# An attention block interleaved with dense products: the order of the score products in each first visit, and the place of one output piece

## The chip, the cores and the metric

The kernel runs on one core of one Trainium2 chip. The metric is the device time of one launch in microseconds; a kernel's time is the median of its runs. TensorE is the matrix engine (PE in the profile, PEld its weight loads), VectorE is DVE, ScalarE is ACT, GpSimd is POOL, and SyncE (SP) issues the DMAs.

## The reference

A pre-normalised transformer layer on 2048 tokens of width 1024, in bfloat16. The attention has 32 heads of 32 columns and a sliding window of 256 keys:

```python
qkv = (x @ wqkv)                      # x here is layernorm(A_x); split into q, k, v by head
scores = einsum("bhqd,bhkd->bhqk", q, k) * (Dh ** -0.5)
mask = (i - j >= 0) & (i - j < 256)
p = softmax(where(mask, scores, -1e9))
h = A_x + einsum("bhqk,bhkd->bhqd", p, v).reshape(B, S, D) @ wo
out = h + silu(layernorm(h) @ w1) @ w2
```

`B_x` is not used: the second half works on `h`.

## The kernel before, in words

The tokens are cut into four blocks of 512. TensorE first makes v, q and k of block 0, then of blocks 1, 2 and 3, then the product with `wo`, then both dense layers of the second half. All of these are groups of eight products of 512 columns, 128 by 128 weights each, which accumulate into one bank of PSUM. Three banks (`four[0]` to `four[2]`) take turns through `next_acc`; a copy on VectorE (line 254 for v, 264 for q and k, an addition on line 285 for `wo`) empties the bank of a finished group. `four[3]`, also called `o_ps`, is kept for the attention's output.

The attention is pushed in between these products. `between` (line 464) is called ahead of each single product and counts them in `self.seen`; two tables written out in `Attention.__init__` say at which count a *visit* or a *piece* comes. From count 256 on there are twelve periods of 48 products. In a period that starts at count t there are:

- three visits, at t+4 (n = 0, the first), t+20 and t+36 (n = 2, the third);
- four pieces, at t+41, t+45, t+59 and t+76. The piece at t+41 is the first of the two behind the third visit, that at t+45 the second; the other two fall into the next period, at its counts 11 and 28.

The order of the program is the order of issue on each engine; the kernel's own schedule is kept.

**A visit** (line 329) makes scores for four heads. Each head has its own strip of 32 rows of the array, and each strip is used in two halves of 64 columns, so eight small products can be under way at once. A head's *own* scores go to the PSUM tile `sc` in parts of 320, 128 and 64 columns. Some heads also stream a second set of 512 columns into a *second bank*: one that is `idle`, the one `behind` (the bank of the group just finished, which VectorE's copy must have emptied) or `out` (`o_ps`, which the normalisation of the piece before must have read). In the first visit heads 0, 1 and 2 have the second banks `idle`, `out` and `behind`, each in four parts of 128 columns (`unit_c`), and head 3 has none. The list `todo` is sorted by `at`, the number of columns that a head has streamed so far, so that the heads advance side by side. There are 48 products in a first visit, 44 in a second and 36 in a third.

ScalarE then takes the exponentials: for the second banks first (line 315 in the first visit), then for `sc` (lines 321 and 322); GpSimd cuts the triangles (line 409).

**A piece** (`attn_piece`, line 442) makes the output of one pair of heads: 24 products of 33 columns into `o_ps` (line 419), and behind them on VectorE the normalisation, a reciprocal (line 430) and a product (line 431) that read `o_ps`. The next piece, and the next second bank `out`, must wait for line 431. Behind a second piece the finished pair is transposed by a DMA on SP (line 439), which `run_late` issues ahead of the next group.

The lines by which a visit builds its order are these:

```python
runs = [(sc[:, h, :], own[half])]
...
at = 0
for bank, parts in runs:
    for p in parts:
        todo.append((at, h, half, bank, p))
        at += p[3] - p[2]
todo.sort(key=lambda m: m[0])
```

Of the kernel before, what the change touches and what calls it, by code (L numbers as in the profile page):

```python
# [47 lines left out]
def kernel(  # L48
# [46 lines left out]
    four = [ps.tile([P, 512], F32, name=f"bank{i}") for i in range(4)]  # L95
# [31 lines left out]
    def xbuf(i):  # L127
        return r_e[:, 3072 + 5120 * (i % 2):5632 + 5120 * (i % 2)]

    def ybuf(i):  # L130
        return r_e[:, 5632 + 5120 * (i % 2):8192 + 5120 * (i % 2)]
# [168 lines left out]
    def unit_xy(i, odd):  # L300
        q0 = odd * P
        mid, first, last = odd, odd - 2, odd + 2
        return [
            [(i, mid, q0, q0 + 320, 64), (i, last, q0 + 256, q0 + 384, 384), (i, first, q0, q0 + 64, 0)],
            [(i, mid, q0 + 64, q0 + 384, 128), (i, first, q0, q0 + 128, 0), (i, last, q0 + 320, q0 + 384, 448)],
        ]

    def unit_c(i):
        pair = (i, i + 1) if (i + 1) % 3 < (i + 2) % 3 else (i + 1, i)
        return [[(ii, kt, q * P, q * P + P, (n * 2 + m) * P)  # L310
                 for n, ii in enumerate(pair) for m, (kt, q) in enumerate(((-1, 0), (2, 3)))]] * 2

    def exp_c(i, h, bank):
        lo, hi = sorted(((i + 1) % 3, (i + 2) % 3))
        nc.scalar.activation(out=c_ring[:, lo:hi + 1:hi - lo, h, :], in_=four[bank].rearrange("p (n q) -> p n q", q=256),  # L315
                             func=ACT.Exp, scale=scale)

    def exp_xy(e, banks, h0, h1):
        tri, mid = banks[:, :, 0:192], banks[:, :, 192:320]
        tri = bass.AP(tensor=tri.tensor, offset=tri.offset, ap=[*tri.ap[:2], [320, 2], tri.ap[2]])  # L320
        nc.scalar.activation(out=tri_of(e)[:, h0:h1, :, 64:256], in_=tri, func=ACT.Exp, scale=scale)  # L321
        nc.scalar.activation(out=full_of(e)[:, h0:h1, :], in_=mid, func=ACT.Exp, scale=scale)

    def select_xy(e, pair):
        four_q = e[:, 1024 * pair:1024 * (pair + 1)].rearrange("p (c q) -> p c q", q=256)
        select(four_q[:, :, 0:P], four_q[:, :, 64:64 + P], False)
        select(four_q[:, :, P:2 * P], four_q[:, :, P:2 * P], True)

    def visit(i, n):


        now = acc_n[0] % 3
        idle, behind, out = (now + 1) % 3, (now + 2) % 3, 3
        if n == 0:
            own, e_own = unit_xy(i, 0), xbuf(i)
            more = [(0, idle, unit_c(i)), (1, out, unit_c(i)), (2, behind, unit_c(i))]
        elif n == 1:
            own, e_own = unit_xy(i, 1), ybuf(i)
            more = [(3, idle, unit_c(i)), (0, out, unit_xy(i + 1, 0)), (1, behind, unit_xy(i + 1, 0))]
        else:  # L340
            own, e_own = unit_xy(i + 1, 1), ybuf(i + 1)
            more = [(2, out, unit_xy(i + 1, 0)), (3, behind, unit_xy(i + 1, 0))]
        todo = []
        for h in range(4):
            for half in range(2):
                runs = [(sc[:, h, :], own[half])]
                for hh, bank, unit in more:
                    if hh == h:
                        runs.append((four[bank], unit[half]))
                at = 0  # L350
                for bank, parts in runs:
                    for p in parts:
# [3 lines that stand above are left out]
        for _, h, half, bank, (ii, kt, qa, qb, col) in todo:  # L356
            b, g = divmod(ii, G)
            t = b * 4 + kt
            r0, k0 = h * DH, (t % 4) * P + half * 64
            nc.tensor.matmul(  # L360
                bank[half * 64:half * 64 + 64, col:col + qb - qa],
                lhsT=kT[t // 4][r0:r0 + DH, g, k0:k0 + 64], rhs=qT[b][r0:r0 + DH, g, qa:qb],
                start=True, stop=True, tile_position=(r0, half * 64),
            )
        side = [h for h, _, unit in more if len(unit[0]) == 3]
        for h, bank, unit in more:
            if h in side:
                exp_xy(xbuf(i + 1), four[bank].rearrange("p (h q) -> p h q", h=1), h, h + 1)
            else:
                exp_c(i, h, bank)  # L370
        if side:
            select_xy(xbuf(i + 1), side[0] // 2)
        exp_xy(e_own, sc[:], 0, 4)
        for pair in range(2):
            select_xy(e_own, pair)

    def scores_0(g, odd):

        q0 = odd * P
        parts = [  # L380
            (odd, 0, q0, q0 + 320, 0), (odd, 1, q0, q0 + 384, 0),
            (odd + 2, 0, q0 + 256, 448, 320), (odd + 2, 1, q0 + 320, 448, 384),
        ]
        if odd:
            parts = [(a, h, f, min(t, 512), c) for a, h, f, t, c in parts[:2]] + [
                (3, 0, 384, 512, 320), (3, 1, 448, 512, 384), (2, 0, 448, 512, 448), (2, 1, 448, 512, 448)]
        for step in range(0, len(parts), 2):
            for hh in range(4):
                for t, half, qa, qb, col in parts[step:step + 2]:
                    r0 = hh * DH  # L390
                    k0 = t * P + half * 64
                    nc.tensor.matmul(  # L392
                        sc[half * 64:half * 64 + 64, hh, col:col + qb - qa],
                        lhsT=kT[0][r0:r0 + DH, g, k0:k0 + 64],
                        rhs=qT[0][r0:r0 + DH, g, qa:qb],
                        start=True, stop=True, tile_position=(r0, half * 64),
                    )
        e = (ybuf if odd else xbuf)(g)[:, 0:2048].rearrange("p (h q) -> p h q", q=512)
        nc.scalar.activation(out=e[:, :, 0:256], in_=sc[:, :, 0:256], func=ACT.Exp, scale=scale)  # L399
        nc.scalar.activation(out=e[:, :, 320:512], in_=sc[:, :, 256:448], func=ACT.Exp, scale=scale)  # L400
        nc.scalar.activation(out=c_ring[:, (g + 1) % 3, :, 128 + 64 * odd:192 + 64 * odd], in_=sc[:, :, 448:512],
                             func=ACT.Exp, scale=scale)
        select(e[:, :, 0:P], e[:, :, 0:P], True)
        select(e[:, :, 256:384], e[:, :, 320:448], False)
        select(e[:, :, 384:512], e[:, :, 384:512], True)
# [42 lines left out]
    class Attention:  # L448


        def __init__(self):
            self.seen = 0
            self.visits, self.pieces = {}, {}
            for d in range(2 * G):
                self.visits[92 + 10 * d] = lambda d=d: scores_0(d // 2, d % 2)
                self.pieces[(122 + 10 * d, 267, 284)[max(d - 13, 0)]] = (d // 2, d % 2)
            for p in range((NB - 1) * G // 2):
                i, t = G + 2 * p, 256 + 48 * p
                for n in range(3):
                    self.visits[t + 4 + 16 * n] = lambda i=i, n=n: visit(i, n)  # L460
                for n in range(4):
                    self.pieces[t + (41, 45, 59, 76)[n]] = (i + n // 2, n % 2)

        def between(self, kt):
            if self.seen in self.pieces:
# [168 lines left out]
    for g0 in range(0, G, 4):  # L634
        for w in range(2):
            for g in range(g0, g0 + 4):
                run_late()
                n = g0 * 2 + w * 4 + g % 4
# [170 lines left out]
```

## Time and profile before

| what | value |
|---|---|
| median of 3 runs | 690.12 us (689.69 to 690.25) |
| time of the profiled execution | 690.01 us |
| its span, first to last instruction | 688.3 us |
| mean granted TensorE clock | 1.000 |
| PE busy | 674.4 us (98% of the span) |
| PEld busy | 338.1 us (49%) |
| DVE busy | 296.0 us (43%) |
| ACT busy | 237.8 us (35%) |
| POOL busy | 155.4 us (23%) |
| first score product of a visit to the last | 90.6 us to 265.7 us |

The span is 1.7 us shorter than the execution's own time; the rest lies ahead of the first and behind the last instruction. A row of a timeline gives the start of its first instruction, the time until the end of its last one, the engine, the line of the kernel, what is written and read, and how many instructions the row merges. A matmul's recorded duration runs from its issue to the end of its passage through the array, so neighbouring matmuls overlap: products of 512 columns last 379 ns in the records and start about 215 ns apart. A few per cent of the matmul records are missing from the trace: behind every score visit but one, and behind the second pieces, one product fewer is recorded than the program has there.

### The profile page before, as it was taken

The numbers are of one execution on the slowest core, as the hardware profiler recorded it, in microseconds if no ns is written. First come the engines' busy times: TensorE is split into PE (matmuls) and PEld (weight loads), VectorE is DVE, ScalarE is ACT, GpSimd is POOL, SyncE is SP. The second block draws the span as 40 slices with busy tenths as digits, with TensorE's granted clock in tenths as the row PEclk, the third lists the DMA queues.
The fourth block names the chain that finished last, engine by engine and source line by source line (L and its number), as shares of the span: only waits on it lengthen the run. The fifth ranks groups of instructions, "written<-read, shape, count | busy, mean of one in ns | idle before, by whom it ended". The sixth has DMA issues, their size and how long they took to land.

```text
span 688.3 us, 14482 instructions
## 1 busy us (share of the span) xinstructions
PE 674.4 (98%) x6099; PEld 338.1 (49%) x6200; DVE 296.0 (43%) x616; ACT 237.8 (35%) x412; POOL 155.4 (23%) x247
## 2 busy tenths in 40 slices
PE   9999999999999999999999999999999999999998
PEld 4445555555555555444444444444444444444445
DVE  5287745774444446733316133343233251333111
ACT  7356666666767664023300033300133100233000
POOL 1046656666676665000000000000000000000000
DMA  8823144124522687765023310023300124100110
GB/s 274 260 53 96 21 59 101 26 42 106 174 78 71 199 283 212 157 244 202 1 87 112 84 39 1 0 92 73 81 1 0 31 87 90 39 1 0 31 38 24
DMA packets 77617, 61.50 MB, mean 89 GB/s; under 512 B 52464, under 2 KB 60656, under 8 KB 77552
## 3 DMA queue, kind: packets, MB, share of 16 engines
q1 hardware_dynamic: 77408, 60.31, 31.3%
q8 instruction: 48, 0.79, 0.5%
q10 hardware_dynamic: 144, 0.26, 0.1%
q14 instruction: 17, 0.14, 0.1%
HBM read 39.85 MB, written 8.39 MB: 70 GB/s over the span
## 4 chain that ended last, share of the span: by engine, by line
PE 97%; issue 2%; DMA 1%; DVE 0%; SPq 0%; ACT 0%; ACTq 0%; DVEq 0%
PE hacc L728 16%; PE bank L262 16%; PE hacc L756 15%; PE bank L756 13%; PE bank L728 12%; PE bank L283 8%; PE bank L252 6%; PE bank L419 5%; PE sc L360 2%; PE bank L360 1%; PE bank L547 1%; PE sc L392 1%; DMA r_w<-in_A_wqkv_dram 1%; PE tp L252 1%; ACT r_e L321 0%
## 5 line engine op out<-in xcount | busy, mean ns | idle before, releaser
L409 POOL TENSOR_SCALAR_AFFINE_SELECT r_e<-r_e 128x512 bf16<-128x512 bf16 x240 | 152.5, 643 | 115.3 <-ACT r_e L399 52.4
L756 PEld LDWEIGHTS <-r_a 128*128 128x128 bf16 x952 | 90.9, 98 | 103.0
L728 PEld LDWEIGHTS <-r_w 128*128 128x128 bf16 x896 | 87.7, 98 | 105.7
L756 PE MATMUL hacc<-r_a 128*128 128x512 bf16 (+2 forms) x523 | 103.2, 356 | 0.5
L756 PE MATMUL bank<-r_a 128*128 128x512 bf16 x412 | 91.4, 379 | 0.5
L728 PE MATMUL hacc<-r_e,r_w 128*128 128x512 bf16 x375 | 84.4, 379 | 0.5
L262 PEld LDWEIGHTS <-r_w 128*128 128x128 bf16 x512 | 45.4, 97 | 49.3 <-issue 1.0
L728 PE MATMUL bank<-r_e,r_w 128*128 128x512 bf16 x284 | 63.9, 379 | 0.1
L264 DVE CAST r_a<-bank 128x512 bf16<-128x512 f32 x58 | 40.1, 691 | 53.9 <-PE bank L262 34.3
L262 PE MATMUL bank<-r_t,r_w 128*128 128x512 bf16 x236 | 57.1, 379 | 2.6 <-issue 2.2
L262 PE MATMUL bank<-r_w 128*128 128x512 bf16 x240 | 56.4, 379 | 1.9 <-issue 1.6
L283 PE MATMUL bank<-r_o,r_a 128*128 128x512 bf16 x242 | 56.4, 379 | 1.5 <-issue 1.1
L419 PEld LDWEIGHTS <-r_e 128*128 128x128 bf16 x1440 | 45.6, 96 | 16.8 <-issue 3.2
L321 ACT ACTIVATE r_e<-sc 128x1536 bf16<-128x1536 f32 x36 | 53.4, 1482 | 0.0
L737 ACT ACTIVATE r_n<-bank 128x512 f32<-128x512 f32 x18 | 10.7, 597 | 117.0 <-PE bank L728 117.0
L419 PE MATMUL bank<-r_a,r_e 128*128 128x33 bf16 x1440 | 46.2, 178 | 0.1
L315 ACT ACTIVATE r_e<-bank 128x512 bf16<-128x512 f32 x48 | 26.1, 597 | 45.0 <-PE bank L360 45.0
L737 ACT ACTIVATE r_n<-hacc 128x512 f32<-128x512 f32 x24 | 14.3, 597 | 75.5 <-PE hacc L728 74.3
L771 DVE SCALAR_TENSOR_TENSOR r_t<-bank,r_t 128x512 bf16<-128x512 f32 x15 | 10.3, 684 | 66.6 <-PE bank L756 66.6
L283 PEld LDWEIGHTS <-r_a 128*128 128x128 bf16 x256 | 23.4, 97 | 25.8
L771 DVE SCALAR_TENSOR_TENSOR r_t<-hacc,r_t 128x512 bf16<-128x512 f32 (+2 forms) x19 | 12.0, 632 | 53.1 <-PE hacc L756 53.1
L252 PE MATMUL bank<-r_w,r_t 128*128 128x512 bf16 x118 | 28.9, 379 | 1.1 <-issue 0.8
(100 smaller groups left out, 574.8 us busy)
## 6 DMA issues: line engine op xcount, KB each, us to landing
r_w<-in_B_w_dram SPq DMA_DIRECT2D x8, 896.0 KB, 6.0
r_a<-in_B_w_dram SPq DMA_DIRECT2D x7, 1024.0 KB, 9.8
r_w<-in_A_wqkv_dram SPq DMA_DIRECT2D x4, 1024.0 KB, 8.3
h_dram<-r_t SPq DMA_DIRECT2D x16, 256.0 KB, 2.8
r_t<-h_dram SPq DMA_DIRECT2D x16, 256.0 KB, 2.9
out_dram<-r_t SPq DMA_DIRECT2D x31, 128.0 KB, 1.7
r_e<-h_dram SPq DMA_DIRECT2D x3, 1024.0 KB, 5.8
r_o<-in_A_x_dram SPq DMA_DIRECT2D x11, 256.0 KB, 5.5
```

Source lines behind the costliest of these rows:

```text
L252: nc.tensor.matmul(acc, lhsT=lnT_b[b % 2][:, kt, j * P:(j + 1) * P], rhs=wv[:, kt, c * 512:(c + 1) * 512], start=(kt == 0), stop=(kt == KT ...
L262: nc.tensor.matmul(acc, lhsT=wqk[:, kt, col0:col0 + P], rhs=lnT_b[b % 2][:, kt, :], start=(kt == 0), stop=(kt == KT - 1))
L264: copy(out=(qT, kT)[which][b][:, g, :], in_=acc)
L283: nc.tensor.matmul(acc, lhsT=qT[b][:, g, j * P:(j + 1) * P], rhs=wo[:, g, c * 512:(c + 1) * 512], start=(g == 0), stop=(g == G - 1))
L315: nc.scalar.activation(out=c_ring[:, lo:hi + 1:hi - lo, h, :], in_=four[bank].rearrange("p (n q) -> p n q", q=256), func=ACT.Exp, scale=scale)
L321: nc.scalar.activation(out=tri_of(e)[:, h0:h1, :, 64:256], in_=tri, func=ACT.Exp, scale=scale)
L409: nc.gpsimd.affine_select(out=dst, in_=src, pattern=[[0, n] for n in dst.shape[1:-1]] + [[sgn, P]], compare_op=ALU.is_ge if upper else ALU ...
L419: nc.tensor.matmul(o_ps[:, qt * 2 + hh, 0:VW], lhsT=chunk_of(i, bank, piece, pair * 2 + hh), rhs=v[:, b * 4 + kt, g * 4 + pair * 2 + hh, : ...
L728: nc.tensor.matmul(acc, lhsT=w1[:, kt, ft * P:(ft + 1) * P], rhs=ln2T[b][:, kt, :], start=(kt == 0), stop=(kt == KT - 1))
L737: nc.scalar.activation(out=th, in_=acc, func=ACT.Tanh, scale=0.5)
L756: nc.tensor.matmul(acc[:, 0:c1 - c0], lhsT=gT[:, ft, j * P:(j + 1) * P], rhs=w2[ft // 4][:, ft % 4, c0:c1], start=(ft == 0), stop=(ft == F ...
L771: nc.vector.scalar_tensor_tensor(out=t_out[j % 2][:, c0:c1], in0=acc[:, 0:c1 - c0], scalar=0.5, in1=t_in[j % 2][:, c0:c1], op0=ALU.mult, o ...
```

## The change

Two places. In a first visit (`n == 0`) the heads whose second bank isn't `behind`, that is heads 0 and 1, put their second bank in front of their own scores; head 2 keeps its own scores first, and so do all heads of the other visits. And the second piece behind a third visit stands one product further on, at t+46 in place of t+45.

```diff
                 for hh, bank, unit in more:
                     if hh == h:
-                        runs.append((four[bank], unit[half]))
+                        runs.insert(0 if n == 0 and bank != behind else 1, (four[bank], unit[half]))
...
                 for n in range(4):
-                    self.pieces[t + (41, 45, 59, 76)[n]] = (i + n // 2, n % 2)
+                    self.pieces[t + (41, 46, 59, 76)[n]] = (i + n // 2, n % 2)
```

The number and the shapes of all instructions stay as they were. The order on VectorE, ScalarE, GpSimd and SP is the same as before; on TensorE the 48 products of each first visit are in another order, and one dense product has changed places with the 24 products of a piece, twelve times.

## The prediction

> **What bounds the kernel now.** I read the page's busy shares and its chain first, then PE's waits, then the timeline of one period.
>
> ```profile
> PE 674.4 (98%) x6099; PEld 338.1 (49%) x6200; DVE 296.0 (43%) x616; ACT 237.8 (35%) x412; POOL 155.4 (23%) x247
> PE 97%; issue 2%; DMA 1%; DVE 0%; SPq 0%; ACT 0%; ACTq 0%; DVEq 0%
> ```
>
> The first row is the page's busy time, the second the chain of work that ended last. TensorE is the bound nearly everywhere: 97% of the chain is PE, and the other engines hardly stand on it. So an edit is worth what it takes from PE's own stream, and a faster exponential or copy is worth nothing unless PE waits for it. The waits of PE's weight loads between 100 and 270 us, where eleven full periods and the end of the twelfth lie, are these:
>
> ```profile
> PEld L360 <- issue: 14.0, 33, 0.4
> PEld L419 <- issue: 3.0, 12, 0.4
> ```
>
> Columns: total us, times, longest. The visits (line 360) have an idle of 0.42 us at each start, 33 times; that is the turn from big products to small ones, and the change leaves the number of turns alone. The pieces (line 419) have an idle 12 times. There are four pieces in each of twelve periods, so one in four is held up. The timeline of PE and DVE shows which, in the period from 160 to 168 us:
>
> ```profile
> 160.89 1.03 PE L262 MATMUL bank<-r_w 128*128 128x512 bf16 x4 [0.16 <-issue]
> 161.75 0.76 PE L419 MATMUL bank<-r_a,r_e 128*128 128x33 bf16 x24
> 162.36 1.02 PE L262 MATMUL bank<-r_w 128*128 128x512 bf16 x4
> 162.62 0.21 DVE L430 RECIPROCAL recip<-bank 128x8 f32<-128x8 f32 x1
> 162.86 0.42 DVE L431 TENSOR_TENSOR r_n<-bank,recip 128x256 bf16<-128x256 f32 x1
> 163.34 0.75 PE L419 MATMUL bank<-r_a,r_e 128*128 128x33 bf16 x24
> 164.13 0.21 DVE L430 RECIPROCAL recip<-bank 128x8 f32<-128x8 f32 x1 [0.84 <-PE bank L419]
> 164.37 0.42 DVE L431 TENSOR_TENSOR r_n<-bank,recip 128x256 bf16<-128x256 f32 x1
> 164.79 0.69 DVE L264 CAST r_a<-bank 128x512 bf16<-128x512 f32 x1
> ```
>
> Four dense products and the first piece: 161.75 - 160.89 = 0.86 us, that is 0.215 each. Four dense products and the second piece: 163.34 - 162.36 = 0.98 us. The 0.12 us more is a wait, and its releaser is on DVE: the normalisation of the first piece ends at 162.86 + 0.42 = 163.28, and the piece that overwrites the same bank starts 0.06 us later. It is the one wait for another engine inside the attention that PE pays for.
>
> **The piece, one product further on.** Removed: the wait. The dense product that now comes ahead starts where the piece would have started, at 162.36 + 4 x 0.215 = 163.22; the piece could then start at 163.44, and needs 163.28 + 0.06 = 163.34. So the wait goes, with 0.10 to spare, and PE gains 0.12. Eleven of the twelve periods look like this one. The other is this:
>
> ```profile
> 117.37 0.81 PE L252 MATMUL bank<-r_w 128*128 128x512 bf16 x3
> 117.80 0.42 DVE L431 TENSOR_TENSOR r_n<-bank,recip 128x256 bf16<-128x256 f32 x1
> 118.28 0.28 PE L419 MATMUL bank<-r_a,r_e 128*128 128x33 bf16 x5
> ```
>
> Without a wait the piece would start at 117.37 + 3 x 0.215 = 118.02; it starts at 118.28, so 0.26 is lost, of which one product recovers 0.21. Sum: 11 x 0.116 (0.12 before rounding) + 0.21 = **1.49 us**. Bounds: 0 if something else holds the piece, and 11 x 0.12 + 0.26 = 1.58 at most.
>
> What is late next: the second piece now ends 163.44 + 0.75 instead of 163.34 + 0.75, 0.10 later, so its normalisation and the copy behind it on DVE (CAST, 164.79 to 165.48) move 0.10 later, to 165.58. Two readers wait for them. One is the bank `behind` in the next first visit, which starts 0.12 earlier than before:
>
> ```profile
> 165.54 0.43 PE L360 MATMUL sc<-r_a 32*64 32x320 bf16 x24
> 165.79 0.47 PE L360 MATMUL bank<-r_a 32*64 32x128 bf16 x24
> 165.54 0.36 PEld L360 LDWEIGHTS <-r_a 32*64 32x64 bf16 x33 [0.42 <-issue]
> 165.54 0.57 PEld L360 LDWEIGHTS <-r_a 32*64 32x64 bf16 x48 [0.42 <-issue]
> 166.26 1.57 ACT L315 ACTIVATE r_e<-bank 128x512 bf16<-128x512 f32 x3 [2.31 <-PE bank L360]
> 166.42 1.46 PE L262 MATMUL bank<-r_w 128*128 128x512 bf16 x6 [0.16 <-issue]
> ```
>
> Its first product stood 29th in the visit's order and was issued at about 165.80; it now stands 33rd, so at 165.80 - 0.12 or a little later, 165.68 against 165.58 + 0.06 = 165.64. That is covered, by some 0.04 us, and more as the 33rd place is later. The other reader is the transposition on SP:
>
> ```profile
> 164.86 1.19 SPq L439 DMA_TRANSPOSE r_a<-r_n  x1
> 166.09 1.32 SPq L225 DMA_TRANSPOSE r_t<-r_o  x1
> ```
>
> It slips by 0.10 with what is queued behind it there, line 225 and loads for a later block; PE needs those a block (24 groups of eight products at 0.215 us, some 40 us) later. I cost both at nothing.
>
> **The visit.** Nothing is added or removed; 48 weight loads and 48 products stand in another order, and in both orders heads 0, 1 and 2 stream 1024 columns. From the first start to the last end this visit takes 165.79 + 0.47 - 165.54 = 0.72 us. The second and third visits have also a longest head of 1024 columns, with 44 and 36 products:
>
> ```profile
> 170.35 0.43 PE L360 MATMUL sc<-r_a 32*64 32x320 bf16 x24
> 170.60 0.41 PE L360 MATMUL bank<-r_a 32*64 32x320 bf16 x20
> 160.08 0.43 PE L360 MATMUL sc<-r_a 32*64 32x320 bf16 x24
> 160.34 0.39 PE L360 MATMUL bank<-r_a 32*64 32x320 bf16 x12
> ```
>
> Both take 0.66 and 0.65 us. So the first visit carries about 0.06 over the pace of the columns, and that is the most to be had: 12 x 0.06 = 0.7 us. One part of it is nearly sure: the old order ends in parts of 128 columns on three heads, the new one in parts of 64 on two, as the second visit does, and half of a 128-column part, at 0.215 us for 512, is 0.027. The other part hangs on how fast the first half runs: it now holds 28 products in place of 24.
>
> ```profile
> L360 PE MATMUL bank<-r_a 32*64 32x128 bf16 x480 | 13.0, 219 | 0.0
> ```
>
> With 0.22 us for one, the last product now starts 0.72 - 0.22 = 0.50 into the visit. The rows of the weight loads show where a visit may run short: 33 loads start within 0.26 us (0.36 less 0.10, the length of one), the other 15 take 0.21 more. If `behind`, whose eight products stand 33rd to 44th in the new order, starts only when the 33rd load has ended, at 0.36, its fourth part starts 3 x 0.054 later, at 0.52, and the last parts of 64 come at 0.54: 0.04 later than now, less the 0.027 of the shorter end, is about +0.015. Between the ends -0.06 and +0.015 I take the middle, which is also little more than the nearly sure part, **-0.02 us**: 12 x 0.02 = **0.24 us** gained.
>
> The Trainium skill, "TensorE: Matmul & The Clock Gate", in the table at its head, gives TensorE a queue of 64 instructions from which weight loads are pulled ahead; 64 would be 32 pairs, and the trace's 33 loads fit it. By that rule the end +0.015 would be the likelier, and the time that of case A below.
>
> The exponentials of the banks `idle` and `out` can start earlier, as their last parts now come at 512 columns: the ACT row at 166.26 waited for PE and would start some 0.2 us sooner. The piece behind that visit has to wait for the exponential of `out`:
>
> ```profile
> 166.85 1.03 PE L262 MATMUL bank<-r_w 128*128 128x512 bf16 x4
> 167.71 0.20 PE L419 MATMUL bank<-r_a,r_e 128*128 128x33 bf16 x2
> ```
>
> Four products and then the piece, again 0.86 us: PE has no wait there today, so an earlier exponential is worth nothing.
>
> **Sum.** 1.49 + 0.24 = 1.73 us less. The profiled execution took 690.01 us, 0.11 under the median; from the median it gives 690.12 - 1.73 = **688.4 us**. From 285 us to the end the view of waits lists none for PE, so the gain should be carried whole.
>
> **The rivals.**
>
> *A, the visit runs out of instructions*: at the end +0.015 the sum is -1.49 + 0.18 = -1.3 us, 688.8. For it: the row of 33 loads. Against: the second visit has mixed parts too and keeps its pace.
>
> *B, a new wait at `behind`*: the cover of 0.04 is thin. If DVE's chain is 0.1 us later than worked out in eleven visits, 1.1 us come back: 689.5. For it: the copy stands right behind the normalisation on DVE (164.37 + 0.42 = 164.79). Against: the old order had 165.79 against 165.48, 0.3 of room.
>
> *C, weight loads that don't overlap, slower than before*: heads 0 and 1 now stream four short parts one after the other in the first half. If a load of 0.10 us could not run beside a product of its own strip, three loads in a row would add 12 x 3 x 0.10 = 3.6 us, and with the piece's 1.49 the time would be 692.2. It decides from about 0.12 us per visit on (1.49 / 12). Against it stands this row:
>
> ```profile
> 165.54 0.16 PEld L360 LDWEIGHTS <-r_a 32*64 32x64 bf16 x16 [0.42 <-issue]
> ```
>
> Within 165.54 to 165.60, where 8 loads serve the first eight parts of 320 columns, 8 more start, for the same eight places, while those parts, 0.215 x 320 / 512 = 0.13 us long, still stream.
>
> The same page of the Trainium skill, Part 3, "The mechanism", says that a weight load overlaps matmuls in flight only when its row group differs; by it case C would come out. The trace disagrees here, by the 16 loads of the row above.
>
> *D, the change doesn't do what it says*: the second piece waits for something that moves with it, such as GpSimd's triangles. Then only the visit is left, 690.12 - 0.24 = 689.9. Against: the 0.06 us between line 431's end and the piece.
>
> **How the numbers follow.** The forecast has 0.62, A 0.14, B 0.08, C 0.10, D 0.06. What a measurement of this kernel can tell from no change is about 0.2%, 1.38 us, so faster means under 688.74 and slower over 691.50. Faster is the forecast alone, 0.62; A, B and D lie within, 0.28; C is slower, 0.10. The range goes from the best visit, 690.12 - 1.58 - 0.7 = 687.8, less 0.4 for the spread of the runs (689.69 to 690.25), to D and its spread, 690.2; C is left out. The forecast's own range is 687.6 to 688.7.
>
> **What would show it.** In the changed profile: the waits of PEld on line 419 drop from 12 to one or none; five dense products and the second piece are 5 x 0.215 = 1.08 us apart; the first visit's span is 0.70, not 0.72, and its last row is one of `sc`; the copy ends about 165.5 with no gap ahead of `behind`; ACT's first row of line 315 starts sooner after the visit. Wrong would be: a gap inside the first visit (B or C), a second piece still late (D), or a first visit of over 0.84 us.

## The result, and the profile after

The changed kernel takes 688.28 us (median of 8 runs, 687.82 to 688.74) against 690.04 us (median of 8) of the kernel before; the ratio is 0.9973, with a 95% interval of 0.9964 to 0.9983. That is 1.76 us less; 1.73 had been forecast. A second series, further down as the last experiment, gave 688.44 us and 0.9978 (0.9963 to 0.9993).

The profiled execution of the changed kernel is the slowest of its 8 runs: 688.74 us, with a span of 687.0 us, only 1.3 less than the span before. The lost part lies ahead of the attention's second stage. The views of lines 360 (visits) and 419 (pieces) give the start of the first and of the last instruction, first for the kernel before, then for the changed one:

```profile
L360 PE MATMUL sc<-r_a x864: 187/214/319, 90.6 to 265.5; 32*64 32x320 bf16 x58, 32*64 32x128 bf16 x58, 32*64 32x64 bf16 x57
L419 PE MATMUL bank<-r_a,r_e x1440: 177/177/180, 48.4 to 277.0; 128*128 128x33 bf16 x180
```

```profile
L360 PE MATMUL sc<-r_a x864: 187/214/319, 91.1 to 264.3; 32*64 32x320 bf16 x59, 32*64 32x64 bf16 x58, 32*64 32x128 bf16 x56
L419 PE MATMUL bank<-r_a,r_e x1440: 177/177/180, 48.8 to 275.7; 128*128 128x33 bf16 x180
```

The first piece already starts 0.4 us later (48.8 against 48.4), before anything that was changed. From the first visit to the last product of a piece it is 277.0 - 90.6 = 186.4 us before and 275.7 - 91.1 = 184.6 us after: 1.8 us less, and that is the change. The busy shares, the chain and the waits of PE's weight loads between 100 and 270 us of the changed kernel:

```profile
PE 683.2 (99%) x6200; PEld 338.4 (49%) x6200; DVE 294.7 (43%) x616; ACT 237.7 (35%) x412; POOL 155.5 (23%) x247
PE 99%; ACT 0%; POOL 0%; issue 0%; DVE 0%; ACTq 0%
PEld L360 <- issue: 14.4, 34, 0.4
PEld L419 <- issue: 0.5, 2, 0.3
```

PE's share rises because this trace holds all 6200 matmul records where the other lacked 101: the four experiments with all records (e1 to e4) have 99% too, the other experiments 98%. With the records the chain's 2% of "issue" is gone as well. The row that counts is the last: 12 waits of pieces, 3.0 us, have become 2, 0.5 us. The same period as in the prediction, on PE, DVE and ACT:

```profile
162.07 1.24 PE L262 MATMUL bank<-r_w 128*128 128x512 bf16 x5
162.57 0.42 DVE L431 TENSOR_TENSOR r_n<-bank,recip 128x256 bf16<-128x256 f32 x1
163.15 0.76 PE L419 MATMUL bank<-r_a,r_e 128*128 128x33 bf16 x24
164.19 0.42 DVE L431 TENSOR_TENSOR r_n<-bank,recip 128x256 bf16<-128x256 f32 x1
164.53 0.68 DVE L264 CAST r_a<-bank 128x512 bf16<-128x512 f32 x1
165.14 0.55 PEld L360 LDWEIGHTS <-r_a 32*64 32x64 bf16 x48 [0.42 <-issue]
165.14 0.25 PE L360 MATMUL bank<-r_a 32*64 32x128 bf16 x4
165.41 0.32 PE L360 MATMUL bank<-r_a 32*64 32x128 bf16 x5
165.60 0.21 PE L360 MATMUL bank<-r_a 32*64 32x128 bf16 x1
165.61 0.20 PE L360 MATMUL sc<-r_a 32*64 32x64 bf16 x2
165.65 1.57 ACT L315 ACTIVATE r_e<-bank 128x512 bf16<-128x512 f32 x3 [1.99 <-PE bank L360]
165.75 1.68 PE L262 MATMUL bank<-r_w 128*128 128x512 bf16 x7
```

Five products and the second piece are 163.15 - 162.07 = 1.08 us apart, five times 0.215: no wait. The normalisation ended at 162.99, 0.16 ahead of the piece. The first visit begins with a second bank, the last products that it issues are `sc`'s, and it takes 165.61 + 0.20 - 165.14 = 0.67 us where it took 0.72. At the trace's full resolution the last product to end is not one of these but a 128-column part of `behind`, the row of 165.60: it ends 0.676 us after the visit's start, the last 64-column part at 0.664. The exponentials start 0.51 us after its start instead of 0.72. The period from one first visit to the next has 14.87 us (the one before this starts at 150.27) instead of 15.02.

### The profile page after: what moved, and what is told of

Its sections match the earlier page's. It is cut to its first block, busy times and chain, and to the rows that moved or that the text cites. A ratio compares the mean times of both kernels' runs of the same rounds, so it can differ in the third digit from the quotient of the medians.

```text
span 687.0 us, 14572 instructions
## 1 busy us (share of the span) xinstructions
PE 683.2 (99%) x6200; PEld 338.4 (49%) x6200; DVE 294.7 (43%) x616; ACT 237.7 (35%) x412; POOL 155.5 (23%) x247
## 4 chain that ended last, share of the span: by engine, by line
PE 99%; ACT 0%; POOL 0%; issue 0%; DVE 0%; ACTq 0%
PE bank L262 17%; PE hacc L728 16%; PE hacc L756 15%; PE bank L756 13%; PE bank L728 12%; PE bank L283 7%; PE bank L252 7%; PE bank L419 5%; PE sc L360 2%; PE bank L360 1%; PE bank L547 1%; PE sc L392 1%; PE tp L252 1%; PE bank L186 0%; ACT r_e L321 0%; POOL r_e L409 0%
## 5 line engine op out<-in xcount | busy, mean ns | idle before, releaser
L262 PE MATMUL bank<-r_t,r_w 128*128 128x512 bf16 x256 | 61.3, 379 | 0.0
L262 PE MATMUL bank<-r_w 128*128 128x512 bf16 x256 | 59.4, 379 | 0.0
L283 PE MATMUL bank<-r_o,r_a 128*128 128x512 bf16 x256 | 58.9, 379 | 0.0
L252 PE MATMUL bank<-r_w,r_t 128*128 128x512 bf16 x128 | 30.5, 380 | 0.0
```

What stands on the lines that cost most here:

```text
L252: nc.tensor.matmul(acc, lhsT=lnT_b[b % 2][:, kt, j * P:(j + 1) * P], rhs=wv[:, kt, c * 512:(c + 1) * 512], start=(kt == 0), stop=(kt == KT ...
L262: nc.tensor.matmul(acc, lhsT=wqk[:, kt, col0:col0 + P], rhs=lnT_b[b % 2][:, kt, :], start=(kt == 0), stop=(kt == KT - 1))
L283: nc.tensor.matmul(acc, lhsT=qT[b][:, g, j * P:(j + 1) * P], rhs=wo[:, g, c * 512:(c + 1) * 512], start=(g == 0), stop=(g == G - 1))
```

## The experiments

Ratios are those to the kernel before on the same chip, with their 95% intervals; "changed" stands for the kernel with both edits.

| run | time, us | ratio (interval) |
|---|---|---|
| e1 visit only | 689.86 | 0.9992 (0.9983 to 1.0001) |
| e2 piece only | 688.74 | 0.9976 (0.9968 to 0.9985) |
| e3 piece at t+44 | 692.13 | 1.0031 (1.0019 to 1.0043) |
| e4 changed, piece at t+47 | 689.14 | 0.9983 (0.9975 to 0.9992) |
| e5 changed, one head | 688.90 | 0.9979 (0.9970 to 0.9988) |
| e6 changed, `behind` first too | 689.32 | 0.9988 (0.9979 to 0.9996) |
| e7 changed, rule in all visits | 688.51 | 0.9977 (0.9965 to 0.9989) |
| e8 changed, piece at t+48 | 692.26 | 1.0035 (1.0022 to 1.0047) |
| e9 wide, old order | 688.14 | 0.9969 (0.9952 to 0.9986) |
| e10 wide, new order | 687.66 | 0.9957 (0.9945 to 0.9969) |
| e11 changed, pieces at t+42, t+46 | 689.61 | 0.9987 (0.9978 to 0.9996) |
| e12 changed again | 688.44 | 0.9978 (0.9963 to 0.9993) |

The kernel before had a median of 690.21 to 690.22 us in the three series.

### The two edits apart: e1 and e2

e1 takes the order of the first visit alone (the piece back to t+45), e2 the piece alone:

```diff
-                    self.pieces[t + (41, 46, 59, 76)[n]] = (i + n // 2, n % 2)
+                    self.pieces[t + (41, 45, 59, 76)[n]] = (i + n // 2, n % 2)
```

> Only the order of the first visit is changed; the second piece stays at t+45. Theory (the wait and the visit are two separate terms, and only the sum of both was measured): each first visit is about 0.04 us shorter from the product before it to the product behind it, 12 x 0.04 = 0.5 us, so about 0.5 us less than before; the 12 idle times ahead of the second pieces stay, about 0.12 us each. Rival (the visit's order is what removes the wait or carries the gain): about 1.8 us less than before. Rival (the order is worth nothing, the gain is all the piece's): within 0.2 us of before.

> Only the second piece is moved, t+45 to t+46; the first visit streams as before. Theory: 11 waits of 0.116 us go and of the one of 0.26 us 0.21 goes, 1.4 to 1.5 us less than before; the first visit takes as long as before (0.50 us from its first to its last product). Rival D (the piece waits for something that moves with it): no change, and the idle time ahead of the second piece stays. Rival B (the copy of the bank behind comes late once the piece is later): less than 1 us gained, with a gap inside the first visit.

The waits of PE's weight loads on line 419 between 100 and 270 us in e1, then in e2, and in e2 one first visit on PE:

```profile
PEld L419 <- issue: 3.3, 13, 0.4
```

```profile
PEld L419 <- issue: 0.2, 1, 0.2
```

```profile
164.95 0.43 PE L360 MATMUL sc<-r_a 32*64 32x320 bf16 x24
165.19 0.47 PE L360 MATMUL bank<-r_a 32*64 32x128 bf16 x24
165.60 1.25 PE L262 MATMUL bank<-r_w 128*128 128x512 bf16 x5
```

With the visit alone all twelve waits stay (and one more has come, below); with the piece alone one is left. From its first product to the next dense one the visit has 165.60 - 164.95 = 0.65 us in the old order, in a trace where that next product is recorded, and 165.75 - 165.14 = 0.61 in the new one. The piece gives 1.5 us by the medians and 1.66 by the ratio (0.9976 of 690.21). The visit gives 0.35 us by the medians and 0.55 by the ratio, with an interval that touches 1, so that the times alone don't rule out an order worth nothing; the rows do, with 0.04 us in each visit. Within these intervals the two add to the 1.76 of both. The rivals "all in the visit" and D (nothing in the piece) are out.

### What the second piece waits for: e3 and e11

e3 is the kernel before with the piece one product earlier, e11 the changed kernel with the first piece one product later, so that the distance of the two is four again while the second stays at t+46:

```diff
-                    self.pieces[t + (41, 45, 59, 76)[n]] = (i + n // 2, n % 2)
+                    self.pieces[t + (41, 44, 59, 76)[n]] = (i + n // 2, n % 2)
```

```diff
-                    self.pieces[t + (41, 46, 59, 76)[n]] = (i + n // 2, n % 2)
+                    self.pieces[t + (42, 46, 59, 76)[n]] = (i + n // 2, n % 2)
```

> The kernel before with the second piece one product earlier, at t+44. Theory (the piece waits for the normalisation of the piece before it, which ends at a fixed time): the wait grows by one product, from 0.12 to 0.33 us, in each of 12 periods: 12 x 0.215 = 2.6 us more than before. Rival D (the wait moves with the piece): no change. Rival (it is the place within a group of eight that matters, not the distance from the first piece): some other amount without an idle time that grows by 0.215 us.

> The changed kernel with the first piece moved one product further on as well, to t+42: the distance of the two is four products again, the second stays at t+46. Theory (the wait is set by the distance to the piece before, since its normalisation ends 1.5 us after its start): 0.12 us per period come back, 12 x 0.12 = 1.4 us more than the changed kernel, less what the later first piece saves where ScalarE's exponential of its bank was late (0.22 us once in the profile of the changed kernel). Rival (the place in the group of eight, t+45 against t+46, is what mattered): as the changed kernel.

PE in one period of e3, then in one of e11:

```profile
162.62 0.81 PE L262 MATMUL bank<-r_w 128*128 128x512 bf16 x3
163.60 0.75 PE L419 MATMUL bank<-r_a,r_e 128*128 128x33 bf16 x24 [0.17 <-DVE r_n L431]
```

```profile
162.32 1.02 PE L262 MATMUL bank<-r_w 128*128 128x512 bf16 x4
163.30 0.75 PE L419 MATMUL bank<-r_a,r_e 128*128 128x33 bf16 x24
```

In e3 the piece starts 0.98 us after the first of three products, 0.33 over 3 x 0.215, and the profile now names the releaser, line 431 on DVE. In e11 it starts 0.98 us after the first of four, the 0.12 of before. So the distance to the first piece sets the wait, by one product's 0.215 us per step until it is used up; the place in the group of eight does not. The times fit this: e3 is 1.9 us over its kernel before where 2.6 was expected (the interval of the ratio, 1.3 to 3.0 us, holds it), and e11 is 1.2 over the changed kernel beside it.

### How much room the bank behind had: e4, e6 and e8

e4 puts the second piece of the changed kernel at t+47, e8 at t+48. e6 lets head 2 stream its second bank `behind` first, too:

```diff
-                        runs.insert(0 if n == 0 and bank != behind else 1, (four[bank], unit[half]))
+                        runs.insert(0 if n == 0 else 1, (four[bank], unit[half]))
```

> The changed kernel with the second piece at t+47. Theory: no wait ahead of the second piece is left, also in the one period where 0.06 us had stayed; the normalisation and the copy behind it come 0.215 us later against the products, and the copy of the bank behind, which in the changed kernel ends 0.20 us ahead of the first product that needs it, now ends 0.02 us after it; with 0.06 us from copy to product, PE waits some 0.08 us inside 11 first visits: 0.9 us more than the changed kernel, about 0.9 us less than before. Rival (the room ahead of the bank is larger than the rows say): as the changed kernel, 1.8 us less than before. Rival (the copy is held up further by the end of the group): over 0.2 us per visit, 2.4 us more than the changed kernel, slower than before.

> The changed kernel, but in the first visit head 2 as well streams its second bank (behind) first. Theory: the first product of that bank is then the fifth of the visit, about 0.01 us after its start, where the copy on VectorE ends 0.07 us after the start of the visit and is seen 0.06 us later: a wait of 0.12 to 0.14 us in 11 first visits, 1.3 to 1.5 us more than the changed kernel, near the time of before. Rival (the wait overlaps with products that run anyway, or the copy is seen sooner): under 0.5 us more.

> The changed kernel with the second piece at t+48, behind the last product of its group, four products ahead of the next first visit. Theory: the copy of the group's bank now goes ahead of the normalisation on VectorE, so the bank behind is ready early; but out, which head 1 now writes as third product of the visit, waits for the normalisation of this piece, which ends some 1.0 to 1.2 us after the piece's end (the copy of 0.69 us stands before it), where the visit starts 4 x 0.215 = 0.86 us after it: a wait of 0.1 to 0.4 us per period, 1.2 to 4 us more than the changed kernel. Rival (the copy does not delay the normalisation): the 0.12 us wait of before in the other place, 1.3 us more than the changed kernel.

One period of e4 on PE and DVE:

```profile
178.66 0.42 DVE L431 TENSOR_TENSOR r_n<-bank,recip 128x256 bf16<-128x256 f32 x1
179.01 0.68 DVE L254 CAST r_a<-bank 128x512 bf16<-128x512 f32 x1
179.40 0.25 PE L360 MATMUL bank<-r_a 32*64 32x128 bf16 x4
179.74 0.24 PE L360 MATMUL bank<-r_a 32*64 32x128 bf16 x2
179.88 0.27 PE L360 MATMUL bank<-r_a 32*64 32x128 bf16 x3
```

The copy ends at 179.69, and the next bank products are issued at 179.74, 0.34 after the visit's start where the changed kernel had its own at 0.27 (165.41 - 165.14). The visit ends at 180.15, 0.75 us after its start, not 0.67: rival B, at work. It costs about 0.07 us in each of eleven visits, 0.8 us in all, and e4 is some 0.7 us slower than the changed kernel by the ratios (0.9983 against 0.9973; the intervals overlap), where 0.9 was expected. So the rows carry this reading, and the times fit it. One first visit of e6:

```profile
164.24 0.68 DVE L264 CAST r_a<-bank 128x512 bf16<-128x512 f32 x1
164.85 0.36 PE L360 MATMUL bank<-r_a 32*64 32x128 bf16 x6
165.18 0.44 PE L360 MATMUL sc<-r_a 32*64 32x320 bf16 x20
```

Its copy ends at 164.92, after the visit's start, and the visit lasts until 165.62: 0.77 us, some 0.09 more than in the changed kernel at full resolution. That is 1.0 us in eleven visits, and the time is 1.0 us over the changed one (the intervals overlap a little): between the theory's 1.3 and the rival's 0.5. So `bank != behind` in the edit is worth about 1 us.

e8 has the expected size, 4 us over the changed kernel, by another way than expected. PE's waits between 100 and 270 us name it, and DVE in one of the three periods shows it:

```profile
PE bank L360 <- DVE r_n L431: 3.6, 3, 1.6
```

```profile
118.30 0.69 DVE L254 CAST r_a<-bank 128x512 bf16<-128x512 f32 x1 [0.63 <-PE bank L252]
118.91 1.28 DVE L193 BATCH_NORM_STATS2 ln_st<-r_o 128x6 f32<-128x512 bf16 x2
120.54 0.42 DVE L431 TENSOR_TENSOR r_n<-bank,recip 128x256 bf16<-128x256 f32 x1
121.02 0.24 PE L360 MATMUL bank<-r_a 32*64 32x128 bf16 x2 [1.11 <-DVE r_n L431]
```

Not a small wait in every period, but three of up to 1.6 us, and none in the others. A piece issued past the end of a group falls behind that group's layer-norm steps on VectorE, too; where these come (two statistics of 0.64 us each here), the visit stands until the normalisation is through. Where there are none, the copy runs beside the piece and costs nothing; that is what the expectation missed.

### What the visit's order saves: e5, e7, e9 and e10

e5 lets head 0 alone stream its second bank first (`n == 0 and bank == idle`), e7 applies the rule to all three visits (`bank != behind`). e9 and e10 replace, in the first visits, the four products of 128 columns of a second bank by two of 256, in the old order and in the new one, with the piece at t+46. These two compute other scores than the reference asks for; only their times are of use:

```diff
+    def unit_w(i):
+        pair = (i, i + 1) if (i + 1) % 3 < (i + 2) % 3 else (i + 1, i)
+        return [[(ii, 2, 2 * P, 4 * P, n * 2 * P) for n, ii in enumerate(pair)]] * 2
...
-            more = [(0, idle, unit_c(i)), (1, out, unit_c(i)), (2, behind, unit_c(i))]
+            more = [(0, idle, unit_w(i)), (1, out, unit_w(i)), (2, behind, unit_w(i))]
```

> The changed kernel, but in the first visit only head 0 (bank idle) streams its second bank first; head 1 and head 2 stream their own scores first. Theory (what the order saves is that the second half of the visit no longer has 24 products of 128 columns on three heads in a row): the second half then has 22 products instead of 20, and the end has 128-column parts of two heads and one 64-column part of head 0; about half of the saving of the visit is kept, 0.02 us per visit, so 0.2 to 0.3 us more than the changed kernel. Rival (only the last part's length counts: 64 instead of 128): head 0's 64 columns are last here too, and the whole saving stays, as the changed kernel.

> The changed kernel with the same rule in all three visits: heads with the second bank idle or out put it first, also in the second visit (heads 3 and 0) and in the third (head 2). Theory (the first visit gained because 48 products came in a poor mixture; the second and third already take the pace of their columns, 0.46 us from first to last product): no gain on PE in these visits, within 0.3 us of the changed kernel; but the bank out is written at the start of the visit, and if the normalisation that reads it is late there, PE waits. Rival (second bank first is better in any visit): 0.02 to 0.04 us less per visit, 24 visits, 0.5 to 1 us less than the changed kernel.

> The piece stays at t+46, the first visit streams in the old order (own scores first), and the second banks of the first visit get their 512 columns in two products of 256 columns per half instead of four of 128: 36 products instead of 48, the same columns. It changes the computation: these columns hold other scores than the reference's. Theory 1 (the old order lost its 0.04 us to the number of short products in a row, case A: products come no faster than one in some 10 ns): the visit takes the pace of its columns, 0.46 us from the first to the last product as the third visit with its 36, and the kernel gains about 12 x 0.04 = 0.5 us against the piece alone, at or under the changed kernel's time. Theory 2 (it lost them to the order itself, to three heads that stream beyond the fourth): the span stays near 0.50 us less what the last parts are longer.

> The same two products of 256 columns per half (the computation is changed in the same way), with the new order and the piece at t+46. Theory 1 (number of products): no difference to the old order with the same products beyond the end, where the last parts are now 64 columns wide; 0.46 us, within 0.3 us of the run beside it. Theory 2 (order): shorter than the old order by some 0.03 us per visit, 0.3 us or more.

A first visit in e9, then in e10 (the scores stand on line 364 there), from the first product to the next dense one:

```profile
164.19 0.43 PE L364 MATMUL sc<-r_a 32*64 32x320 bf16 x24
164.43 0.42 PE L364 MATMUL bank<-r_a 32*64 32x256 bf16 x12
164.78 1.69 PE L262 MATMUL bank<-r_w 128*128 128x512 bf16 x7
```

```profile
164.03 0.30 PE L364 MATMUL bank<-r_a 32*64 32x256 bf16 x4
164.04 0.33 PE L364 MATMUL sc<-r_a 32*64 32x320 bf16 x4
164.60 1.68 PE L262 MATMUL bank<-r_w 128*128 128x512 bf16 x7
```

With the same columns in 36 products the old order takes 164.78 - 164.19 = 0.59 us instead of 0.65, and the new one 0.57 instead of 0.61. So cutting the same columns into more and shorter products cost 0.06 and 0.04 us, and the order is worth 0.04 us at 48 products and 0.02 at 36. Theory 1 is right about the greater part of the excess; it isn't all, since an order effect stays. The weight loads show where the time goes. In all twelve first visits of the old order the last 15 of the 48 loads start one every 8.3 ns, from 0.35 to 0.47 us after the visit's start, where the loads before them come mostly in groups some 3 ns apart. In the changed kernel this slow stretch holds only the last 11 loads (0.36 to 0.45 us), in e5 the last 13, in e9 the last 3, and in e10 there is none. It begins at 0.35 to 0.36 us wherever there is one, but not at a fixed count of loads (load 34, 38 or 36 in the visits of 48 products); what sets it no run here shows. The times lie in this order, too (e9 2.1 us under its kernel before, e10 2.6); the 0.5 us between them are more than twelve times 0.02, but the intervals of the two overlap.

e5 lies between: 1.45 us under the kernel before, 0.4 over the changed one by the ratios, whose intervals overlap. Its visit, which starts at 164.83, ends with this row:

```profile
165.33 0.21 PE L360 MATMUL bank<-r_a 32*64 32x128 bf16 x1
```

It lasts 165.33 + 0.21 - 164.83 = 0.71 us, so of the 0.04 us only 0.01 is kept, not half, and 12 x 0.03 = 0.4 us is lost. In the order of the program e5's last part has 64 columns, but the last to start and to end is one of 128. So e5 doesn't test the rival of the last part's length, and no other run tests it by itself. e7 is no faster than the changed kernel, and its second and third visits last 0.65 us as there: where 44 and 36 products already keep the pace of the columns, their order is worth nothing. (Its time alone, with an interval of 0.9965 to 0.9989, would not rule out the rival's 0.5 us.)

### A late exponential that came with the new order: e12

> The changed kernel once more, unchanged, beside the other three. Expected: 1.7 to 1.8 us less than before. Asked of its profile: does the one first piece near 250 us again start one product's time (0.22 us) late, behind an exponential that starts some 0.3 us later than in other periods? If it is the same place again, it belongs to the kernel; if not, it is a chance event of one execution.

The changed kernel's profile has one first piece that is late. The exponential ahead of it (the first ACT row) and PE around it, near 250 us:

```profile
249.00 0.43 PE L360 MATMUL sc<-r_a 32*64 32x320 bf16 x24
249.58 1.25 PE L283 MATMUL bank<-r_o,r_a 128*128 128x512 bf16 x5
250.18 0.49 ACT L321 ACTIVATE r_e<-bank 128x384 bf16<-128x384 f32 x1 [1.70 <-POOL r_e L409]
250.89 0.75 PE L419 MATMUL bank<-r_a,r_e 128*128 128x33 bf16 x24
```

From the first of five products to the piece it is 1.31 us, 0.22 more than the 1.09 of the other periods. The exponential starts 1.18 us after the visit's start; in the period before it (visit at 234.13) it is 0.88. e12 repeats it at the same place, and in e2, with the old order, it isn't there:

```profile
249.41 0.49 ACT L321 ACTIVATE r_e<-bank 128x384 bf16<-128x384 f32 x1 [1.70 <-POOL r_e L409]
249.69 0.10 PEld L419 LDWEIGHTS <-r_e 128*128 128x128 bf16 x1
250.12 0.53 PE L419 MATMUL bank<-r_a,r_e 128*128 128x33 bf16 x15
```

```profile
249.95 0.49 ACT L321 ACTIVATE r_e<-bank 128x384 bf16<-128x384 f32 x1 [1.42 <-PE bank L360]
```

It is no chance event: the late exponential stands in this eleventh period in all ten profiles with the new order in the first visit (in e7 without a cost to PE, in e5 with 0.15 us of it), and in none of the four with the old one (before, e2, e3, e9). What delays it stays open. The profile names GpSimd, but the last of GpSimd's triangles that could have released it was done 0.14 to 0.21 us earlier, at no fixed distance in the ten. In e11, where the first piece stands one product later, it costs PE less than 0.02 us.

## Why the prediction was right

- **The piece**: right in place and size. The wait was the normalisation's (e3, e11), it went in eleven periods, and 0.06 us of the twelfth's 0.26 stayed (in the changed kernel, in the period near 118 us). Forecast 1.49; e2 measured 1.66 with an interval of 1.0 to 2.2.
- **The cover ahead of `behind`**: right that it holds, wrong in size. The step "so its normalisation and the copy behind it on DVE (CAST, 164.79 to 165.48) move 0.10 later" failed. In the kernel before the copy waited for the last product of its group on PE, not only for the normalisation ahead of it: that product's record ends at 164.75, and the copy starts at 164.79. In the changed kernel the product ends at 164.35, well ahead of the copy at 164.53, which follows the normalisation alone. So the copy slipped less: the visit started 0.06 us after the copy's end before (165.54 and 165.48) and 0.07 ahead of it after (165.14 and 165.21), a shift of 0.13, not 0.22. With `behind` at 165.41 the room was 0.20 less the 0.06 of the semaphore, 0.14, and not 0.04. e4 shows that one product more is too much.
- **The visit**: the sum came out, by two errors that nearly cancel, and that is luck. The visit became 0.04 us shorter, not 0.02: 12 x 0.04 = 0.5. The 0.02 was the middle of two ends, little more than a shorter last part that was called "nearly sure"; but the last product to end still has 128 columns, and it ends earlier because it starts earlier (0.46 us after the visit's start, not 0.50). Against this stands the 0.22 us of the late exponential. The step "PE has no wait there today, so an earlier exponential is worth nothing" had weighed an earlier exponential only as a gain, and only behind the first visit. 0.5 - 0.2 is the 0.3 that 0.24 was forecast for. That the total came within 0.03 us is luck as well: the interval of the 1.76 goes from 1.2 to 2.5.
- **Rival A** was right that many short products cost time (e9, e10), but the old order suffered from it more than the new one: 15 loads in the slow stretch, then 11. That a queue which runs out is the reason is not shown. **C** is out: a first half with 28 products and four short parts per head did not lengthen the visit (0.67 us, 0.72 before). By the Trainium skill, "TensorE: Matmul & The Clock Gate", Part 3, "The mechanism", it should have; no run here agrees. **B** and **D** are told above: B begins one product further on, D is out.

## What to carry to other kernels

On an engine that is busy without a gap, a wait of a tenth of a microsecond in each of twelve periods is found by counting starts: four products and a piece took 0.98 us in one place and 0.86 in another. The cheapest cure is to move work that needs nothing in front of the waiting instruction, by just as many steps as the wait is long; each step more takes a product's time from the room of whoever reads behind it (here one product was right, two gave some 0.7 us of it back, and three, past the end of the group, made the kernel slower than before). Move one edge at a time, and look for what stands between the two on the other engine's queue.

## What was not expected of the hardware

The span of concurrent small products does not depend on the columns of the longest row strip alone: the same 1024 columns took 0.65 us in 48 products and 0.59 in 36, in the same order. It isn't the count alone either: the second visits, with 44 products in another mixture, take 0.59 us too. And a store can hold up the matrix engine from afar. In the profiled execution of e5, the slowest of that kernel's, the addition on DVE waited for an earlier store of the same buffer, and a third visit stood for over 2 us:

```profile
264.37 0.69 DVE L285 TENSOR_TENSOR r_t<-bank,r_a 128x512 bf16<-128x512 f32 x1 [5.25 <-DMA h_dram<-r_t]
265.68 0.32 PE L360 MATMUL bank<-r_a 32*64 32x320 bf16 x2 [1.32 <-DVE r_n L431]
```

The other profiles show no stall of that length there (e7, e9 and e10 have one of 0.3 to 0.6 us, behind an addition that waited for such a store), so part of the scatter of the runs, as the 687.82 to 688.74 us of the changed kernel, may come from such DMAs; that was not tested.
